# Earlier softmax sums and a copy of h in step 23 of 32: one change to a three-stage kernel on one core

## The chip, the cores and the metric

The kernel runs on one core of a Trainium2 chip. The metric is device time in microseconds (us), the median of several runs. The engines of the core work side by side, each through its own queue in order: TensorE (PE; its weight loads are shown as PEld), VectorE (DVE), ScalarE (ACT), GpSimd (POOL) and SyncE (SP), which issues most of the DMAs. An instruction that waits for a semaphore holds up all that is queued behind it on its engine.

## What is computed

```
# attention: 4 batches, 8 heads, 576 positions, head size 64; float32
scores = q @ k.T / 8                      # heads 0-3: the last 32 positions; heads 4-7: every 32nd
attn   = exp(scores - max); attn /= sum(attn) + 1e-9
x      = attn @ v                         # -> 2304 tokens x 512
# first feed forward
h = x @ w_in;  g = h * cos(h);  x = g @ w_out         # 512 -> 2048 -> 512
# second feed forward
h = x @ w_in2; g = P(h) / Q(h); out = g @ w_out2      # P cubic, Q quadratic
```

## The kernel before

The attention of one batch is cut into two halves of 288 positions, so there are eight halves, n = 0 to 7 in the code (the first to the eighth). Each half has four pairs of heads, i = 0 to 3. The scores of a pair lie on 128 partitions in five blocks: 445 columns in all for pairs 0 and 1, 315 or 630 for pairs 2 and 3 (630 in odd n).

The first feed forward runs in blocks of tokens, and a block in 16 steps, one for each 128 of the 2048 hidden columns. Steps are counted by `g` over the whole kernel; the first feed forward has g = 0 to 127, the second g = 128 to 223. Up to g = 47 the blocks are 256 or 352 tokens wide, from g = 48 on 288. While a block is worked on, the attention of a later half is worked in beside it: half n (from 2 on) has its stages in the steps after `s0 = 16*(n-1)`.

In step g, PE computes h of that step in a PSUM bank (`l1`, L409: 12 matmuls). There are two banks for h, so that L409 of step g+2 needs all readers of the h of step g to be done. Then come the letters of a string that sets the order in which the other engines' instructions are issued; the string of a step is in `ORD` or, for g = 48 to 111, in `C_ORD[g % 32]`. Letters in capitals U, K, V belong to h of step g, and N, M, G, H to step g-1:

- U (L498, ACT): t = h/2pi + 1/4, rounded to an integer. t has two buffers, so that U of step g+2 waits until H of step g has read t.
- K (L504, ACT): `hs`, a copy of h in SBUF; k (L506) does it on DVE. A step without K has none.
- V (L508, DVE): u = h/2pi - t.
- N (L510, ACT): the sine of u. M (L512, DVE): t = u * hs, or u * h, straight from the bank, in a step without a copy.
- G (L516, ACT): gh, the rounded high part of t. H or h (L518, on POOL or on DVE): gl = t - gh.
- T: the transposes (L345, PE) of a pair of heads and their copies `pt` to SBUF (L353, ACT). L: the "late" work planned for this step.

After the letters, PE does the second matmul for step g-3 (`l2`, L428: 12 matmuls, needs gh and gl of that step), and then, for a pair transposed in this step, probabilities times v (`att_o`, L364), which needs `pt`. So PE's queue in a step with a pair is L409, L345, L428, L364.

The late work of a step holds, in this order, decoding of the second feed forward's weights (L143 on ACT, two steps on L596, L157 and L603 on DVE, two instructions each) and then attention: the maximum, the exponential, and the sum and normalisation of a pair. A sum is three instructions on DVE (L287 over the columns, L334 and L335 on five columns), a normalisation one on POOL (L336). The table `TABE` (even n) or `TABO` (odd n), for n from 3 on (n = 2 has a table of its own, `TAB2`), has a row for each pair; its last three entries are the steps, counted from s0, of the exponential, of sum and normalisation, and of transpose and product with v:

```
TABO = [[-4, -2, -1, 0, 4, 9, 11], [-3, -1, 0, 1, 6, 10, 12], [-2, 12, 2, 3, 4, 11, 13], [1, 13, 4, 5, 6, 12, 14]]
```

Five halves use these two tables: n = 3 (sums in steps 41 to 44, transposes in 43 to 46), 4 (57 to 60, 59 to 62), 5 (73 to 76, 75 to 78), 6 (89 to 92, 91 to 94) and 7 (105 to 108, 107 to 110).

Of the kernel before, what the change touches and what calls it, by code (L numbers as in the profile page):

```python
# [45 lines left out]
TAB = ((-4, -2, -1, 0, 6, 9, 11), (-3, -1, 0, 1, 6, 10, 12), (0, 12, 2, 3, 6, 11, 13), (1, 13, 4, 5, 6, 12, 14))  # L46
TAB2 = TABE = TABO = TAB
W2RD = (5, 7, 2)
# [9 lines left out]
C_ORD = {}  # L58
# [22 lines left out]
BLAG = 8  # L81
START = ['cst ACT', 'lq 0 0', 'lq 0 2 ACT', 'load 2 0', 'lv 0 1', 'lv 0 3 w0', 'lq 0 3', 'lq 0 1 ACT', 'load 0 0', 'lv 0 0', 'load 0 1', 'load 1 0 ACT', 'load 1 1', 'warm 38', 'lv 0 2 w0', 'masks', 's 0 0 y', 's 0 1 y', 's 0 2 y', 's 0 3 y', 'lq 1 0', 'ab', 'lq 1 2', 'lq 1 1', 'load 2 1', 'load 3 0', 'load 3 1', 'red 0 0', 'lv 1 0', 'exps 0 0', 'lq 1 3', 'ms 0 1', 'ex 0 1', 'red 0 2', 'lv 1 1', 'exps 0 2', 'norm 0 0 POOL', 'ms 0 3', 'ex 0 3', 'load 4 1', 'sum 0 1', 'norm 0 2 POOL', 'norm 0 1 POOL', 'sum 0 3', 'warm 29', 'abs 0 0', 'abs 0 1', 't 0 0 h', 'load 4 0', 'te 0 0', 'd 0 0 0', 'norm 0 3 POOL', 'o 0 0', 'd 0 1 0', 'd 0 0 1', 'd 0 1 1', 'd 0 0 2', 'd 0 1 2', 't 0 1 y', 'abs 1 1', 'te 0 1', 'oe 0 0', 'split 0 1 POOL', 'abs 1 0', 't 0 2 h', 'o 0 1', 'd 1 1 0', 'd 1 1 1', 'd 1 0 0', 'te 0 2', 'load 6 1', 'd 1 0 1', 'split 0 0 POOL', 'd 1 0 2', 't 0 3 y', 'oe 0 1', 's 1 0 y', 'te 0 3', 'd 1 1 2', 'o 0 2', 'split 1 0 POOL', 'oe 0 2', 'split 1 1 POOL', 'o 0 3', 's 1 1 y', 'abs 2 0', 'abs 2 1 DVE', 'd 2 0 0', 'd 2 1 0', 'abs 3 0', 'd 2 0 1', 'd 2 1 1', 'abs 3 1', 's 1 2 y', 's 1 3 a', 'red 1 0', 'd 2 1 2', 'red 1 1', 'd 2 0 2', 'exps 1 0', 'oe 0 3', 'split 2 0 POOL', 'exps 1 1', 'red 1 2', 'split 2 1 POOL', 'd 3 1 0', 'red 1 3', 'exps 1 2', 'exps 1 3', 'd 3 0 0', 'd 3 0 1', 'd 3 1 1', 'd 3 0 2', 'd 3 1 2', 'split 3 0 POOL', 'load 5 0', 'load 5 1', 'load 7 0', 'split 3 1 POOL DVE', 'load 7 1', 'load 6 0', 'next']
LV1 = [2, 4]
TABE = [[-5, -2, -1, 0, 4, 9, 11], [-3, -1, 0, 1, 6, 10, 12], [0, 12, 2, 3, 6, 11, 13], [1, 13, 4, 5, 6, 12, 14]]
TABO = [[-4, -2, -1, 0, 4, 9, 11], [-3, -1, 0, 1, 6, 10, 12], [-2, 12, 2, 3, 4, 11, 13], [1, 13, 4, 5, 6, 12, 14]]
C_ORD.update({0: 'swNMUKjVGHTL', 1: 'swNMUjVGhTL', 2: 'swNMUKjVGhTL', 3: 'swNMUKjVGhTL', 4: 'swNMUKjVGhTL', 5: 'swNMUKjVGhTL', 6: 'swNMUKjVGhTL', 7: 'swNMUkjVGHTL', 8: 'swNMUKjVGHTL', 9: 'swNMUKjVGHTL', 10: 'swNMUKJVGhTL', 11: 'swNMUKjVGhTL', 12: 'swNMUKjVGhTL', 13: 'swNMUKjVGhTL', 14: 'swNMUKjVGHTL', 15: 'swNMUKjVGHTL', 16: 'swNMUKjVGHTL', 17: 'swNMUKjVGhTL', 18: 'swNMUKjVGhTL', 19: 'swNMUKjVGhTL', 20: 'swNMUKjVGHTL', 21: 'swNMUKjVGhTL', 22: 'swNMUKjVGhTL', 23: 'swNMUjVGhTL', 24: 'swNLMUKjVGHT', 25: 'wNsMUKjVGHTL', 26: 'swNMUKjVGhTL', 27: 'swNMUKjVGhTL', 28: 'swNMUKjVGhTL', 29: 'swNMUKjVGhTL', 30: 'swNMUKjVGHTL', 31: 'swNMUKjVGHTL'})
W2RD = [4, 6, 2]
X2RD = [4, 2, 2]

# [2 lines left out]
def attention_moe_moe_kernel(ctx: ExitStack, tc: tile.TileContext, qk0, qk, vv, w1, w2, consts, a, b, out):  # L92
# [455 lines left out]
    def plan(kind, g, fn, *args):  # L548
        plans[kind].setdefault(g, []).append((fn, args))
# [5 lines left out]
    def plan_attention(p):  # L555
        for n in range(1, 2 * B):
            s0 = NF * (n - 1)
            if n == 1:
# [6 lines left out]
                continue  # L565
            for i, (lq, lv, ss, ms, xs, us, ts) in enumerate(TAB2 if n == 2 else (TABE, TABO)[n % 2]):
                if lq is not None:
# [164 lines left out]
    with tc.manual_schedule():  # L732
        with tc.tile_pool(name="att", bufs=2) as p:
# [87 lines left out]
            for kind, g, cmd in PL1:  # L821
                plan(kind, g, do, cmd)
            plan("late", 2 * NF + TABO[0][4], roots)
            plan_w2(p)
# [98 lines left out]
```

## Time and profile before

| what | us |
|---|---|
| median of three runs (972.56 to 974.1) | 972.74 |
| the profiled execution, its own time | 970.86 |
| span of that execution in the trace | 969.1 |
| PE busy | 917.1 (95%) |
| DVE busy | 712.1 (73%) |
| ACT busy | 690.8 (71%) |
| POOL busy | 291.5 (30%) |

The span is the stretch from the first to the last instruction that the trace shows. PE is busy nearly all of it, and its granted clock is full (a nine or more in tenths) from the second of 40 slices on. The shares are means over stages: the start up to about 90 us, the first feed forward with attention beside it to about 545 us, the second feed forward after it.

### The profile page before, as it was taken

How to read it: one execution, taken by the hardware profiler on the slowest of the kernel's cores; microseconds unless marked ns; L12 is line 12 of the kernel's file. 1: busy time of each engine (PE TensorE's matmuls, PEld its weight loads, DVE VectorE, ACT ScalarE, POOL GpSimd, SP SyncE). 2: the span in 40 equal slices, each digit the busy share in tenths (PEclk: the TensorE clock that was granted, in tenths of full speed). 3: DMA queues.
4: the chain of work that ended last, by engine and by line, in shares of the span. 5: the costliest groups of instructions: out<-in, count | busy, mean ns of one | idle time of the engine just before them, and what ended most of it. 6: DMA issues, size and time to landing. Idle time of an engine off the chain costs nothing.

```text
span 969.1 us, 17280 instructions
## 1 busy us (share of the span) xinstructions
PE 917.1 (95%) x6367; PEld 857.2 (88%) x6367; DVE 712.1 (73%) x1337; ACT 690.8 (71%) x1453; POOL 291.5 (30%) x279
## 2 busy tenths in 40 slices
PE   7578999999999999999999999999999999999997
PEld 6467999989989989999899988898898898898895
DVE  5998745685665676656758788778778787787776
ACT  5987765665674865657658877777777777777875
POOL 2577722132222122221313123232232233232221
PEclk9799999999999999999999999999999999999999
DMA  9766103434324344344236320010100200100000
GB/s 312 265 222 211 45 2 119 163 107 150 113 101 154 104 144 141 131 146 139 93 104 190 120 73 0 12 55 1 58 9 1 66 1 1 66 1 0 33 1 33
DMA packets 51525, 89.35 MB, mean 92 GB/s; under 512 B 4584, under 2 KB 28400, under 8 KB 51440
## 3 DMA queue, kind: packets, MB, share of 16 engines
q1 hardware_dynamic: 50720, 86.58, 27.2%
q10 hardware_dynamic: 720, 1.67, 0.5%
q8 instruction: 50, 0.82, 0.3%
q14 instruction: 35, 0.29, 0.1%
HBM read 70.40 MB, written 17.83 MB: 91 GB/s over the span
## 4 chain that ended last, share of the span: by engine, by line
PE 38%; DVE 22%; ACT 21%; POOL 11%; issue 5%; DMA 2%; POOLq 0%; SPq 0%; ACTq 0%; DVEq 0%
PE h L409 17%; PE y L428 16%; POOL z L468 9%; DVE r L471 7%; ACT r L467 6%; ACT r L466 5%; ACT gh L477 5%; DVE h L472 3%; DVE a L472 3%; PE a L249 2%; DVE dec L157 2%; PE a L364 2%; DMA qk<-in_qk_dram 2%; PE a L345 1%; DVE t L512 1%
## 5 line engine op out<-in xcount | busy, mean ns | idle before, releaser
L409 PE MATMUL h<-xh,w 128*128 128x288 f32 (+3 forms) x1408 | 338.6, 312 | 14.1 <-DVE t L512 11.8
L409 PEld LDWEIGHTS h<-xh,w 128*128 128x128 f32 x1408 | 245.3, 191 | 19.3 <-DVE t L512 13.1
L428 PE MATMUL y<-gh,w 128*128 128x288 f32 (+2 forms) x1024 | 229.1, 300 | 0.6 <-ACT w L163 0.6
L409 PE MATMUL h<-xl,w 128*128 128x288 f32 (+3 forms) x704 | 207.1, 310 | 0.0
L428 PE MATMUL y<-w,gh 128*128 128x512 f32 x576 | 195.9, 393 | 5.5 <-DVE ev L442 4.6
L468 POOL TENSOR_TENSOR z<-q,r 128x384 f32<-128x384 f32 x96 | 97.3, 1013 | 297.9 <-ACT r L467 287.8
L428 PEld LDWEIGHTS y<-gh,w 128*128 128x128 f32 x1024 | 172.0, 189 | 0.8 <-ACT w L163 0.8
L428 PE MATMUL y<-gl,w 128*128 128x288 f32 (+2 forms) x512 | 151.6, 296 | 2.2 <-POOL gl L518 2.1
L409 PEld LDWEIGHTS h<-xl,w 128*128 128x128 f32 x704 | 134.8, 191 | 1.8
L428 PEld LDWEIGHTS y<-w,gh 128*128 128x128 f32 x576 | 108.1, 188 | 28.0 <-DVE ev L442 7.1
L471 DVE SCALAR_TENSOR_TENSOR r<-z,r 128x384 f32<-128x384 f32 x96 | 69.5, 724 | 73.9 <-POOL z L468 73.9
L518 POOL TENSOR_TENSOR gl<-t,gh 128x288 fp32r<-128x288 f32 (+2 forms) x67 | 67.2, 1003 | 184.5 <-ACT gh L516 162.4
L498 ACT ACTIVATE t<-h,biases 128x288 int32<-128x288 f32 (+2 forms) x116 | 57.6, 497 | 89.1 <-PE h L409 78.7
L428 PE MATMUL y<-w,gl 128*128 128x512 f32 x288 | 114.7, 398 | 5.1 <-DVE gl L482 5.0
L508 DVE SCALAR_TENSOR_TENSOR u<-h,t 128x288 f32<-128x288 f32 (+2 forms) x128 | 58.2, 455 | 76.5 <-ACT hs L504 60.8
L409 PE MATMUL a<-xh,w 128*128 128x384 f32 x384 | 106.3, 337 | 0.0
L428 PEld LDWEIGHTS y<-gl,w 128*128 128x128 f32 x512 | 97.0, 189 | 3.0 <-POOL gl L518 2.9
L516 ACT ACTIVATE gh<-t 128x288 fp32r<-128x288 f32 (+2 forms) x128 | 56.6, 442 | 29.3 <-DVE t L512 27.4
L510 ACT ACTIVATE u<-u,biases 128x288 f32<-128x288 f32 (+2 forms) x128 | 67.8, 530 | 12.9 <-DVE u L508 12.6
L409 PEld LDWEIGHTS a<-xh,w 128*128 128x128 f32 x384 | 70.5, 188 | 1.8
L428 PEld LDWEIGHTS y<-w,gl 128*128 128x128 f32 x288 | 54.0, 188 | 20.0 <-DVE gl L482 12.0
L512 DVE TENSOR_TENSOR t<-u,hs 128x288 f32<-128x288 f32 (+1 forms) x91 | 50.5, 555 | 25.6 <-ACT u L510 25.1
(115 smaller groups left out, 1601.1 us busy)
## 6 DMA issues: line engine op xcount, KB each, us to landing
raw<-in_w_dram SPq DMA_DIRECT2D x63, 512.0 KB
qk<-in_qk_dram SPq DMA_DIRECT2D x18, 481.0 KB
wf<-dec SPq DMA_DIRECT2D x32, 256.0 KB
wf<-wf SPq DMA_DIRECT2D x32, 256.0 KB
x2s<-x2d SPq DMA_DIRECT2D x24, 192.0 KB
out_dram<-ev SPq DMA_DIRECT2D x17, 256.0 KB
v<-in_vv_dram SPq DMA_DIRECT2D x16, 240.0 KB
v<-in_vv_dram SPq DMA_DIRECT2D x24, 157.5 KB
```

Of the source, the lines that this page charges most:

```text
L409: PE.matmul(h[:, :n], w[d["ph"], f, 0][:, 128 * c:128 * c + 128], x[c][:, cs], start=k == 0, stop=k == len(ops) - 1)
L428: PE.matmul(y, l, r, start=first and i == 0 and bk != bB, stop=last and i == 2 and bk != bA)
L467: ACT.activation(out=r, in_=r, func=AF.Exp, scale=-1.0, bias=biases[:, 1:2])
L468: POOL.tensor_tensor(out=z, in0=q, in1=r, op=ALU.mult)
L471: DVE.scalar_tensor_tensor(out=r, in0=z, scalar=2.0, in1=r, op0=ALU.subtract, op1=ALU.mult, reverse0=True)
L472: DVE.scalar_tensor_tensor(out=h, in0=h, scalar=ab[:, 0:1], in1=r, op0=ALU.add, op1=ALU.mult)
L498: ACT.activation(out=k, in_=h, func=AF.Identity, scale=INV_2PI, bias=biases[:, 2:3])
L508: DVE.scalar_tensor_tensor(out=u, in0=h, scalar=INV_2PI, in1=k, op0=ALU.mult, op1=ALU.subtract)
L510: ACT.activation(out=u, in_=u, func=AF.Sin, scale=TWO_PI, bias=biases[:, 3:4])
L512: DVE.tensor_tensor(out=t, in0=u, in1=e.get("hs", h), op=ALU.mult)
L516: ACT.activation(out=e["gh"], in_=t, func=AF.Copy)
L518: (POOL if c == "H" else DVE).tensor_tensor(out=e["gl"], in0=t, in1=e["gh"].bitcast(F32), op=ALU.subtract)
```

## The change

Two things are changed, both in tables that set the order; no instruction is added but one copy in each of two steps.

```diff
-TABE = [[-5, -2, -1, 0, 4, 9, 11], [-3, -1, 0, 1, 6, 10, 12], [0, 12, 2, 3, 6, 11, 13], [1, 13, 4, 5, 6, 12, 14]]
-TABO = [[-4, -2, -1, 0, 4, 9, 11], [-3, -1, 0, 1, 6, 10, 12], [-2, 12, 2, 3, 4, 11, 13], [1, 13, 4, 5, 6, 12, 14]]
+TABE = [[-5, -2, -1, 0, 4, 7, 11], [-3, -1, 0, 1, 6, 8, 12], [0, 12, 2, 3, 6, 9, 13], [1, 13, 4, 5, 6, 10, 14]]
+TABO = [[-4, -2, -1, 0, 4, 7, 11], [-3, -1, 0, 1, 6, 8, 12], [-2, 12, 2, 3, 4, 9, 13], [1, 13, 4, 5, 6, 10, 14]]
 C_ORD.update({
...
-  23: 'swNMUjVGhTL',
+  23: 'swNMUKjVGhTL',
...
 })
```

The sixth entry of each row falls by two: 20 sums and 20 normalisations (five halves, n = 3 to 7, of four pairs) are issued two steps sooner, while exponentials and transposes stay. `C_ORD[23]` is used at g = 55 and g = 87 alone, the only steps with g % 32 = 23 between 48 and 111; step 119 has a string of its own in `ORD`.

VectorE in half n = 5, from V of step 71 on. Before:

```order
L508 SCALAR_TENSOR_TENSOR u<-h,t 128x288
L512 TENSOR_TENSOR t<-u,hs 128x288
L508 SCALAR_TENSOR_TENSOR u<-h,t 128x288
L596 TENSOR_SCALAR dec<-dec 128x512 x2
L157 SCALAR_TENSOR_TENSOR dec<-raw,dec 128x512 x2
L512 TENSOR_TENSOR t<-u,hs 128x288
L508 SCALAR_TENSOR_TENSOR u<-h,t 128x288
L603 SCALAR_TENSOR_TENSOR dec<-raw,dec 128x512 x2
L287 TENSOR_REDUCE sm<-p 128x5
L334 TENSOR_SCALAR sm<-sm 128x5
L335 RECIPROCAL sm<-sm 128x5
```

After, from the same V of step 71 on:

```order
L508 SCALAR_TENSOR_TENSOR u<-h,t 128x288
L287 TENSOR_REDUCE sm<-p 128x5
L334 TENSOR_SCALAR sm<-sm 128x5
L335 RECIPROCAL sm<-sm 128x5
L512 TENSOR_TENSOR t<-u,hs 128x288
L508 SCALAR_TENSOR_TENSOR u<-h,t 128x288
L596 TENSOR_SCALAR dec<-dec 128x512 x2
L157 SCALAR_TENSOR_TENSOR dec<-raw,dec 128x512 x2
L287 TENSOR_REDUCE sm<-p 128x5
L334 TENSOR_SCALAR sm<-sm 128x5
L335 RECIPROCAL sm<-sm 128x5
```

The sums of pairs 0 and 1, which stood behind the L603 pair and one step later, now stand in front of M of step 71 and of M of step 72; those of pairs 2 and 3 take their old places in steps 73 and 74. Half n = 7 has the same order.

VectorE in half n = 4, from the weight decoding of step 56 on. Before:

```order
L596 TENSOR_SCALAR dec<-dec 128x512 x2
L157 SCALAR_TENSOR_TENSOR dec<-raw,dec 128x512 x2
L512 TENSOR_TENSOR t<-u,h 128x288
L508 SCALAR_TENSOR_TENSOR u<-h,t 128x288
L512 TENSOR_TENSOR t<-u,hs 128x288
```

After, from the first sum, which is issued at the end of step 55, on:

```order
L287 TENSOR_REDUCE sm<-p 128x5
L334 TENSOR_SCALAR sm<-sm 128x5
L335 RECIPROCAL sm<-sm 128x5
L596 TENSOR_SCALAR dec<-dec 128x512 x2
L157 SCALAR_TENSOR_TENSOR dec<-raw,dec 128x512 x2
L287 TENSOR_REDUCE sm<-p 128x5
L334 TENSOR_SCALAR sm<-sm 128x5
L335 RECIPROCAL sm<-sm 128x5
L512 TENSOR_TENSOR t<-u,hs 128x288
```

M of step 55 reads the copy `hs` in place of the bank `h`, and has two sums in front of it (step 56 has L ahead of M in its string, so its decoding and its sum come first). Half n = 6, step 87, has the same order.

GpSimd in half n = 5, a piece of the difference:

```order
-L518 TENSOR_TENSOR gl<-t,gh 128x288 x3
-L336 TENSOR_TENSOR p<-p,sm 128x445 x2
+L518 TENSOR_TENSOR gl<-t,gh 128x288
+L336 TENSOR_TENSOR p<-p,sm 128x445
+L518 TENSOR_TENSOR gl<-t,gh 128x288
+L336 TENSOR_TENSOR p<-p,sm 128x445
+L518 TENSOR_TENSOR gl<-t,gh 128x288
```

The normalisations of pairs 0 and 1 now stand between the gl of steps 70, 71 and 72 instead of behind all three.

## Rows read from the trace of the kernel before

**Rows 1.** The page, first part: busy us (share of the span) x instructions.

```profile
PE 917.1 (95%) x6367; PEld 857.2 (88%) x6367; DVE 712.1 (73%) x1337; ACT 690.8 (71%) x1453; POOL 291.5 (30%) x279
```

**Rows 2.** Waits of PE, 200 to 545 us: who waited for whom, total us, times, longest.

```profile
PE h L409 <- DVE t L512: 3.8, 2, 1.9
PE a L345 <- POOL p L336: 2.7, 2, 1.4
...
PE a L364 <- ACT pt L353: 1.0, 1, 1.0
```

**Rows 3.** Timeline, half 3: start us, length us, instruction [idle before it, releaser].

```profile
218.68 1.24 POOL L336 TENSOR_TENSOR p<-p,sm 128x630 f32<-128x630 f32 x1 [1.93 <-DVE sm L335]
219.88 1.23 POOL L518 TENSOR_TENSOR gl<-t,gh 128x352 fp32r<-128x352 f32 x1
...
221.14 0.56 ACT L498 ACTIVATE t<-h,biases 128x352 int32<-128x352 f32 x1 [2.96 <-POOL gl L518]
...
222.85 0.80 PE L364 MATMUL a<-pt,v 89*64 89x58 f32 x20 [1.02 <-ACT pt L353]
```

**Rows 4.** Timeline of PE, half 4: first L409 of step 57, and L364 of pair 0.

```profile
274.14 0.40 PE L409 MATMUL h<-xh,w 128*128 128x288 f32 x1 [1.89 <-DVE t L512]
...
284.40 0.80 PE L364 MATMUL a<-pt,v 89*64 89x58 f32 x20
```

**Rows 5.** Timeline of PE, half 5: transposes of pair 0 and its L364.

```profile
344.91 0.78 PE L345 MATMUL a<-cst,p 128*89 128x128 f32 x5 [1.36 <-POOL p L336]
...
347.39 0.80 PE L364 MATMUL a<-pt,v 89*64 89x58 f32 x20
```

**Rows 6.** Timeline of DVE, half 5 (the first row from step 68).

```profile
321.95 0.76 DVE L596 TENSOR_SCALAR dec<-dec 128x512 int32<-128x512 int32 x2
...
336.59 0.46 DVE L512 TENSOR_TENSOR t<-u,hs 128x288 f32<-128x288 f32 x1 [1.31 <-ACT u L510]
...
337.65 1.37 DVE L596 TENSOR_SCALAR dec<-dec 128x512 int32<-128x512 int32 x2
...
342.69 0.60 DVE L287 TENSOR_REDUCE sm<-p 128x5 f32<-128x445 f32 x1
...
343.64 0.43 DVE L512 TENSOR_TENSOR t<-u,hs 128x288 f32<-128x288 f32 x1
...
346.05 0.43 DVE L512 TENSOR_TENSOR t<-u,hs 128x288 f32<-128x288 f32 x1
...
347.51 0.80 DVE L287 TENSOR_REDUCE sm<-p 128x5 f32<-128x630 f32 x1
...
348.67 0.46 DVE L376 TENSOR_TENSOR xl<-a,xh 128x288 fp32r<-128x288 f32 x1
349.10 1.33 DVE L512 TENSOR_TENSOR t<-u,hs 128x288 f32<-128x288 f32 x1
```

**Rows 7.** Timeline of ACT, half 5: copies pt of pair 0.

```profile
346.87 0.74 ACT L353 ACTIVATE pt<-a 89x384 f32<-89x384 f32 x2
```

**Rows 8.** Timeline of POOL, half 5: one gl, and the normalisation of pair 2.

```profile
337.70 1.02 POOL L518 TENSOR_TENSOR gl<-t,gh 128x288 fp32r<-128x288 f32 x1 [1.76 <-PE h L409]
...
348.88 1.24 POOL L336 TENSOR_TENSOR p<-p,sm 128x630 f32<-128x630 f32 x1 [1.61 <-DVE sm L335]
```

**Rows 9.** Timeline of DVE, half 4: steps 56 and 57.

```profile
271.53 0.98 DVE L596 TENSOR_SCALAR dec<-dec 128x512 int32<-128x512 int32 x2
...
273.64 0.45 DVE L512 TENSOR_TENSOR t<-u,h 128x288 f32<-128x288 f32 x1
...
276.93 0.46 DVE L508 SCALAR_TENSOR_TENSOR u<-h,t 128x288 f32<-128x288 f32 x1 [1.11 <-ACT hs L504]
```

**Rows 10.** Timeline of POOL and ACT, half 4: gl of 55, U of 57, pt of pair 0.

```profile
274.69 0.81 POOL L518 TENSOR_TENSOR gl<-t,gh 128x288 fp32r<-128x288 f32 x1 [9.47 <-ACT gh L516]
...
276.09 0.50 ACT L498 ACTIVATE t<-h,biases 128x288 int32<-128x288 f32 x1 [1.07 <-PE h L409]
...
283.41 0.75 ACT L353 ACTIVATE pt<-a 89x384 f32<-89x384 f32 x2
```

More of the change, by code (lines that the diff above doesn't have):

```diff
@@ L83 @@
 LV1 = [2, 4]
-TABE = [[-5, -2, -1, 0, 4, 9, 11], [-3, -1, 0, 1, 6, 10, 12], [0, 12, 2, 3, 6, 11, 13], [1, 13, 4, 5, 6, 12, 14]]
-TABO = [[-4, -2, -1, 0, 4, 9, 11], [-3, -1, 0, 1, 6, 10, 12], [-2, 12, 2, 3, 4, 11, 13], [1, 13, 4, 5, 6, 12, 14]]
-C_ORD.update({0: 'swNMUKjVGHTL', 1: 'swNMUjVGhTL', 2: 'swNMUKjVGhTL', 3: 'swNMUKjVGhTL', 4: 'swNMUKjVGhTL', 5: 'swNMUKjVGhTL', 6: 'swNMUKjVGhTL', 7: 'swNMUkjVGHTL', 8: 'swNMUKjVGHTL', 9: 'swNMUKjVGHTL', 10: 'swNMUKJVGhTL', 11: 'swNMUKjVGhTL', 12: 'swNMUKjVGhTL', 13: 'swNMUKjVGhTL', 14: 'swNMUKjVGHTL', 15: 'swNMUKjVGHTL', 16: 'swNMUKjVGHTL', 17: 'swNMUKjVGhTL', 18: 'swNMUKjVGhTL', 19: 'swNMUKjVGhTL', 20: 'swNMUKjVGHTL', 21: 'swNMUKjVGhTL', 22: 'swNMUKjVGhTL', 23: 'swNMUjVGhTL', 24: 'swNLMUKjVGHT', 25: 'wNsMUKjVGHTL', 26: 'swNMUKjVGhTL', 27: 'swNMUKjVGhTL', 28: 'swNMUKjVGhTL', 29: 'swNMUKjVGhTL', 30: 'swNMUKjVGHTL', 31: 'swNMUKjVGHTL'})
+TABE = [[-5, -2, -1, 0, 4, 7, 11], [-3, -1, 0, 1, 6, 8, 12], [0, 12, 2, 3, 6, 9, 13], [1, 13, 4, 5, 6, 10, 14]]
+TABO = [[-4, -2, -1, 0, 4, 7, 11], [-3, -1, 0, 1, 6, 8, 12], [-2, 12, 2, 3, 4, 9, 13], [1, 13, 4, 5, 6, 10, 14]]
+C_ORD.update({0: 'swNMUKjVGHTL', 1: 'swNMUjVGhTL', 2: 'swNMUKjVGhTL', 3: 'swNMUKjVGhTL', 4: 'swNMUKjVGhTL', 5: 'swNMUKjVGhTL', 6: 'swNMUKjVGhTL', 7: 'swNMUkjVGHTL', 8: 'swNMUKjVGHTL', 9: 'swNMUKjVGHTL', 10: 'swNMUKJVGhTL', 11: 'swNMUKjVGhTL', 12: 'swNMUKjVGhTL', 13: 'swNMUKjVGhTL', 14: 'swNMUKjVGHTL', 15: 'swNMUKjVGHTL', 16: 'swNMUKjVGHTL', 17: 'swNMUKjVGhTL', 18: 'swNMUKjVGhTL', 19: 'swNMUKjVGhTL', 20: 'swNMUKjVGHTL', 21: 'swNMUKjVGhTL', 22: 'swNMUKjVGhTL', 23: 'swNMUKjVGhTL', 24: 'swNLMUKjVGHT', 25: 'wNsMUKjVGHTL', 26: 'swNMUKjVGhTL', 27: 'swNMUKjVGhTL', 28: 'swNMUKjVGhTL', 29: 'swNMUKjVGhTL', 30: 'swNMUKjVGHTL', 31: 'swNMUKjVGHTL'})
 W2RD = [4, 6, 2]
```

## Prediction

> **What bounds the kernel now.** PE is busy for 95% of the span [rows 1], so the first view to read is what PE waited for in the stretch that the change touches, 200 to 545 us [rows 2]. Five waits there can be moved by it: two of L409 for M (L512), 3.8 us together, two of the transposes L345 for the normalisation on POOL, 2.7 us, and one of L364 for its copies pt, 1.0 us. The timelines then tell where each lies. (Halves are named by the code's n.) In half 3 it is the L364 of pair 1 [rows 3]; in halves 4 and 6 the L409 of steps 57 and 89 [rows 4]; in halves 5 and 7 the transposes of pair 0 [rows 5]. Together 1.0 + 3.8 + 2.7 = 7.5 us, which is the most that the change can gain. The next view is the timeline of DVE at the same places, since both edits alter what is queued there. In half 5 it goes without a gap from 337.65 us to 349.10 us: M of step 73 at 343.64, M of step 74 at 346.05, and the copies pt of pair 0 follow M of step 74 by 0.82 us, because in ACT's queue they stand behind G of step 74 [rows 6, 7]. PE's L364 starts 0.52 us after these copies start [rows 5, 7]. So at this place two chains run side by side to the same L364: POOL's normalisation, which is late, and DVE's queue, which is hardly earlier.
>
> **The price of a sum.** From its L287 to the next instruction on DVE a sum takes 343.64 - 342.69 = 0.95 us for 445 columns and 348.67 - 347.51 = 1.16 us for 630 [rows 6]. The sums of 315 columns in even halves I take at the nearest row, 0.95 us less 0.1. None is added; what counts is which M they are put in front of.
>
> **The copy.** One more L504 on ACT in steps 55 and 87. It frees the h bank at V instead of at M, so the wait of 1.89 us [rows 4] goes. Its own price, about 0.3 us on ACT, is hidden: M of step 55, which waits for what is behind it on ACT, is late by more for another reason (below).
>
> **Half 3.** The wait of 1.02 us comes from POOL: gl of step 42 at 219.88 stood behind a normalisation that ran from 218.68 to 219.92, and U of step 44 waited 2.96 us for that gl; the copies pt, and with them L364, are queued behind [rows 3]. After the change this normalisation is issued two steps sooner, gl no longer has its 1.24 us in front of it, and U and the copies can come sooner by about that, more than the 1.02 us that PE waits. The sums go into steps 39 to 42, where DVE still has idle time. I count -1.0 us; bounds 0 and -1.02.
>
> **Halves 5 and 7, step by step.** The normalisation of pair 0 will be done several us ahead (two steps, at 3 us each), so the transposes no longer wait: -1.36 us at L345. But L364 behind them still needs the copies, these need G, and that needs M of step 74. Before, M of step 74 had two sums of pairs 0 and 1 in front of it within DVE's gapless stretch (2 x 0.95). After, four sums are in front of it. The first falls into the idle 1.31 us before M of step 71 [rows 6], the other three do not: 0.95 + 1.16 + 1.16 = 3.27 us against 1.90 us. M of step 74, its G, the copies and L364 come 1.37 us later, L364 at 348.76 us instead of 347.39. PE waits there for the copies; the time saved at L345 is inside that wait, and the net is **+1.37 us** if nothing else is lost. That is the lower bound.
>
> To it comes what DVE and POOL take from each other. M at 349.10 took 1.33 us instead of 0.43 to 0.46, and it ended just after the normalisation that ran on POOL from 348.88 to 350.12; the L596 pair took 1.37 us beside a gl on POOL (337.70 to 338.72), and 0.76 us without one [rows 6, 8]. So an instruction of DVE that meets one on POOL loses some 0.6 to 0.9 us. After the change the first normalisation starts about 336.4 us and meets M of step 71 at 336.6, which is then held for about the rest of it, some 0.75 us; DVE had 1.06 us from that M to its L596 pair, for two instructions of which V needs 0.46 us at most, so I leave 0.45 us of it. The other moved normalisations stand beside L603 and beside gl of step 73 on DVE; I count one further loss of 0.6 us. That gives 1.37 + 0.45 + 0.6 = **+2.4 us** for each of the two halves. If each meeting costs in full it is +2.8 us. The value taken lies nearer the upper end because the rows show the loss at every meeting that I looked at.
>
> The Trainium skill states a rule for this (SBUF — State Buffer, section "SBUF: two separate sides"): VectorE and GpSimd share a pair of SBUF ports by an exclusive lock, which a VectorE instruction with two SBUF inputs needs too, and the one that comes second is held for the whole of the first. By that rule alone each meeting costs in full, +2.8 us here and +1.3 us in halves 4 and 6, and the whole sum would be +7.2 us, 979.9 us; with no such lock it would be the lower ends, 975.4 us. The trace agrees where it can: M with u and hs both in SBUF was held to the end of the normalisation, 1.33 us.
>
> **Halves 4 and 6, step by step.** M of step 55 was at 273.64 us [rows 9]. After, two sums stand in front of it, 1.90 us, of which 0.22 us falls into the wait for ACT that is inside the 0.98 us of the L596 pair (0.76 us without): +1.68 us. M's result goes on through G on ACT, gl on POOL (274.69 + 0.81 = 275.50 us, 1.86 us after M) and then U of step 57, which needs the buffer t that gl reads, and V of step 57, 0.84 us after U [rows 9, 10]. So V of step 57 cannot come sooner than about 2.75 us after M of step 55: 273.64 + 1.68 + 2.75 = 278.07 us, against 276.93 us before [rows 9], +1.14 us. From there to M of step 58 the same work is queued (sums of 315 in place of 445 columns, -0.2 us), so that the copies pt, at 283.41 us before [rows 10], come at 284.35 us and L364 0.52 us later, at 284.87 us against 284.40 us [rows 4]. The wait of 1.89 us is gone and yet the net is **+0.5 us**: PE waits at L364, in part already at L409 of step 58 for V of step 56, which also stands behind both sums. If the L596 pair meets the normalisation of pair 0 (+0.6 us) and gl of step 55 waits 0.2 us behind that of pair 1, it is +1.3 us. Taken: **+1.0 us** each, nearer the upper end for the same reason. A lower bound far off is -1.89 us, if V of step 57 did not depend on M of step 55 in this way.
>
> After these places nothing follows: in the steps up to the next half PE had no waits, and DVE has two sums less in the steps that come behind, so a delay of PE stays as it is. DMAs are not moved; in SP's queue only names of buffers differ.
>
> **Sum.** -1.0 + 2 x 1.0 + 2 x 2.4 = +5.8 us. On the profiled execution: 970.86 + 5.8 = 976.7 us. The median of the three runs is 1.9 us above that execution, and I put the sum on the median: 972.74 + 5.8 = 978.5 us. With all lower ends: -1.0 + 1.0 + 2.7 = +2.7 us, 975.4 us. With all upper ends, half 3 at nothing: 2.6 + 5.6 = +8.2 us, 980.9 us.
>
> **Rivals.**
> *All five waits go and nothing comes instead*: -7.5 us, 965.2 us. This is what holds if DVE has enough slack to take the sums sooner. For it: DVE is busy for only 73% of the span [rows 1], and half 3 is such a place. Against it: DVE's queue in half 5 has no gap for eleven us, and L364 waits for the copies whatever the normalisation does.
> *The copy pays, the sums at best break even*: in halves 4 and 6 the idle time of DVE around V of step 57 (1.11 us before it [rows 9]) takes the sums, and -3.8 us is kept; in halves 5 and 7 the wait only changes its place, from L345 to L364, at the same end. -1.0 - 3.8 + 0 = -4.8 us, 967.9 us. It decides for faster if M of step 74 comes no later than before, that is, if three sums cost no more there than two did. For it: before the change the L596 and L603 pairs lose time to POOL already, and this could go away.
> *Little net*: halves 5 and 7 at +1.4 us, halves 4 and 6 at 0, half 3 -1.0 us: +1.7 us, 974.4 us.
> That the change does not do what it says is excluded by the order of the instructions; it does less in one respect, since step 23 of 32 occurs only twice.
>
> **How the numbers follow.** A measurement of this kernel can tell about 0.2%, 1.95 us, from no change. Forecast, slower by more than that: 0.75. Little net: 0.11. Copy pays: 0.08. All gained: 0.06. So faster 0.14, same 0.11, slower 0.75. The range reaches from just below the rival at 967.9 us to 981.5 us, a little above the sum of the upper ends; outside it lies the rival at 965.2 us and what of the forecast goes beyond.
>
> **What the profile of the changed kernel would show.** Waits of PE: none for L512 and none for the normalisation L336, and in their place waits of L364 for ACT's pt, about 3.8 us (2.4 + 1.36) in halves 5 and 7 each, and waits of L409 for DVE's V (L508) and of L364 for pt in halves 4 and 6, about 2.9 us together in each. On DVE four sums end before M of step 74, and some M (L512) beside a normalisation take over a microsecond. In half 3 no wait of L364. I am wrong if L364 in halves 5 and 7 waits less than 1.4 us (then M of step 74 was not late), or if PE waits at neither place.

## The result, and the profile after

The changed kernel takes 981.79 us (median of five runs, 980.79 to 982.67) where the kernel before takes 972.56 us beside it: 1.0094 times as long, 95% interval 1.0080 to 1.0108, or +9.2 us. Slower was forecast, at +5.8 us with an upper end of 981.5 us; the measured time lies 0.3 us above that end. The profiled execution took 980.79 us, its span is 979.0 us.

What PE waited for from 200 to 560 us in the kernel after (total us, times, longest), in answer to [rows 2]:

```profile
PE a L364 <- ACT pt L353: 9.6, 4, 3.5
PE h L409 <- DVE u L508: 4.3, 4, 1.4
PE a L249 <- DVE t L512: 0.3, 1, 0.3
```

The waits for M (L512 at L409) and for the normalisation (L336 at L345) are gone, and the copies pt (L353) have taken their place, with V (L508) at L409. Of the 4.3 us, 1.4 us are the wait ahead of the first moved sum, which was there before. Where the waits lie is shown by the timeline of PE after, in halves 3, 4 and 5, in answer to [rows 3 to 5]:

```profile
221.43 0.80 PE L364 MATMUL a<-pt,v 89*64 89x58 f32 x20
...
275.34 0.40 PE L409 MATMUL h<-xh,w 128*128 128x288 f32 x1 [1.36 <-DVE u L508]
...
283.84 0.80 PE L364 MATMUL a<-pt,v 89*64 89x58 f32 x20 [1.34 <-ACT pt L353]
...
343.13 0.71 PE L345 MATMUL a<-cst,p 128*89 128x128 f32 x5
...
348.87 1.32 PE L364 MATMUL a<-pt,v 89*64 89x58 f32 x20 [3.45 <-ACT pt L353]
...
350.53 0.44 PE L409 MATMUL h<-xl,w 128*128 128x288 f32 x1
...
353.17 1.27 PE L345 MATMUL a<-cst,p 128*89 128x128 f32 x5
```

In half 3 L364 of pair 1 has no wait left. In half 4 one wait of 1.89 us has become two, 1.36 and 1.34 us. In half 5 the transposes no longer wait and L364 does, for 3.45 us. And then something that no term of the prediction held: the same twenty L364 take 1.32 us in place of 0.80 us, and an L409 of 288 columns 0.44 us in place of 0.29 us. The windows of this stretch give the reason (us; busy us of PE, PEld, DVE, ACT and POOL with their instructions; PEclk, the granted clock; DMA share; GB/s):

```profile
345.00:349.00 4.00, 0.55 (x6) 0.32 (x6) 3.65 (x9) 2.70 (x7) 2.39 (x2) 0.86 0.99 339
349.00:351.00 2.00, 2.00 (x23) 1.90 (x24) 0.70 (x2) 0.85 (x3) 0.07 (x1) 0.50 0.29 115
...
353.20:356.00 2.80, 2.80 (x18) 2.77 (x17) 0.82 (x2) 2.59 (x7) 0.00 (x0) 0.73 0.05 12
356.00:360.00 4.00, 4.00 (x46) 3.80 (x45) 1.28 (x4) 2.37 (x7) 0.00 (x0) 1.00 0.37 100
```

PE comes out of its wait at a granted clock of 0.50, the lower of the two levels (1.2 GHz), and is back at 1.00 only about six us later (354.6 us, from the lengths of the matmuls). From L364 of pair 0 to L364 of pair 1 it took 352.03 - 347.39 = 4.64 us before and takes 356.14 - 348.87 = 7.27 us now: 2.6 us more. In half 7 it is 488.88 - 481.28 = 7.60 us against 4.65 us, 2.95 us more.

The whole account comes from the start of the last L364 of each half, before and after:

| half | before | after | behind by | made in this half | forecast |
|---|---|---|---|---|---|
| (first L364 of half 3) | 216.45 | 216.12 | -0.33 | | |
| 3 | 233.49 | 232.06 | -1.43 | -1.10 | -1.0 |
| 4 | 298.29 | 297.72 | -0.57 | +0.86 | +1.0 |
| 5 | 361.34 | 365.40 | +4.06 | +4.63 | +2.4 |
| 6 | 424.76 | 429.92 | +5.16 | +1.10 | +1.0 |
| 7 | 487.76 | 498.14 | +10.38 | +5.22 | +2.4 |

The five halves add up to +10.7 us. With the -0.3 us ahead of them and -0.5 us behind them this is the difference of the two spans, 979.0 - 969.1 = 9.9 us, where the medians differ by 9.2 us.

In half 5, 3.45 - 1.36 = 2.09 us of the 4.63 us is longer waiting, and the other 2.5 us is the lower clock. In half 7 the waits at L409 and L364 give 0.25 + 3.47 - 1.36 = 2.36 us, and the clock 2.9 us.

DVE after, half 5, in answer to [rows 6], with two normalisations from POOL's timeline; behind it, from ACT's timeline, the copies:

```profile
334.26 0.45 DVE L508 SCALAR_TENSOR_TENSOR u<-h,t 128x288 f32<-128x288 f32 x1
334.63 0.61 DVE L287 TENSOR_REDUCE sm<-p 128x5 f32<-128x445 f32 x1
...
336.02 0.46 DVE L512 TENSOR_TENSOR t<-u,hs 128x288 f32<-128x288 f32 x1
336.07 1.20 POOL L336 TENSOR_TENSOR p<-p,sm 128x445 f32<-128x445 f32 x1 [0.40 <-DVE sm L335]
...
341.30 2.27 DVE L603 SCALAR_TENSOR_TENSOR dec<-raw,dec 128x512 int32<-128x512 int32 x2
343.48 0.80 DVE L287 TENSOR_REDUCE sm<-p 128x5 f32<-128x630 f32 x1
...
344.86 1.30 POOL L336 TENSOR_TENSOR p<-p,sm 128x630 f32<-128x630 f32 x1 [1.84 <-DVE sm L335]
345.57 0.90 DVE L518 TENSOR_TENSOR gl<-t,gh 128x288 fp32r<-128x288 f32 x1
346.39 0.80 DVE L287 TENSOR_REDUCE sm<-p 128x5 f32<-128x630 f32 x1
...
347.54 0.43 DVE L512 TENSOR_TENSOR t<-u,hs 128x288 f32<-128x288 f32 x1
...
348.35 0.74 ACT L353 ACTIVATE pt<-a 89x384 f32<-89x384 f32 x2
```

M of step 74 (347.54) comes behind four sums, the copies 0.81 us behind it, L364 0.52 us behind these, as forecast. In half 4 the chain M, G, gl, U, V of steps 55 to 57 runs as forecast too, at DVE and ACT:

```profile
274.50 0.42 DVE L512 TENSOR_TENSOR t<-u,hs 128x288 f32<-128x288 f32 x1
...
276.50 0.51 ACT L498 ACTIVATE t<-h,biases 128x288 int32<-128x288 f32 x1 [0.65 <-POOL gl L518]
...
277.34 0.46 DVE L508 SCALAR_TENSOR_TENSOR u<-h,t 128x288 f32<-128x288 f32 x1 [0.56 <-ACT hs L504]
```

V of step 57 comes 2.84 us after M of step 55 (2.75 us in the prediction, and 0.2 us for a normalisation in front of gl).

### The profile page after: what moved, and what is told of

The parts are those of the page before. It is cut to its first block, busy times and chain, and to the rows that moved or that the text cites. A ratio compares the mean times of both kernels' runs of the same rounds, so it can differ in the third digit from the quotient of the medians.

```text
span 979.0 us, 17265 instructions
## 1 busy us (share of the span) xinstructions
PE 922.3 (94%) x6367; PEld 862.5 (88%) x6367; DVE 714.3 (73%) x1337; ACT 691.7 (71%) x1455; POOL 292.1 (30%) x279
## 4 chain that ended last, share of the span: by engine, by line
PE 36%; DVE 24%; ACT 22%; POOL 10%; issue 5%; DMA 1%; POOLq 0%; SPq 0%; DVEq 0%; ACTq 0%
PE h L409 16%; PE y L428 14%; POOL z L468 9%; DVE r L471 7%; ACT r L467 6%; ACT r L466 5%; ACT gh L477 5%; DVE h L472 3%; DVE a L472 3%; DVE dec L157 2%; PE a L249 2%; PE a L364 2%; DMA raw<-in_w_dram 1%; PE a L345 1%; DVE t L512 1%
## 5 line engine op out<-in xcount | busy, mean ns | idle before, releaser
L409 PE MATMUL h<-xh,w 128*128 128x288 f32 (+3 forms) x1408 | 340.3, 313 | 13.7 <-DVE t L512 8.6
L409 PEld LDWEIGHTS h<-xh,w 128*128 128x128 f32 x1408 | 246.3, 192 | 19.4 <-DVE t L512 9.3
L409 PE MATMUL h<-xl,w 128*128 128x288 f32 (+3 forms) x704 | 207.6, 311 | 0.0
L409 PEld LDWEIGHTS h<-xl,w 128*128 128x128 f32 x704 | 135.4, 192 | 1.8
L518 POOL TENSOR_TENSOR gl<-t,gh 128x288 fp32r<-128x288 f32 (+2 forms) x67 | 66.6, 995 | 191.5 <-ACT gh L516 173.9
L508 DVE SCALAR_TENSOR_TENSOR u<-h,t 128x288 f32<-128x288 f32 (+2 forms) x128 | 58.2, 455 | 79.0 <-ACT hs L504 63.7
L409 PE MATMUL a<-xh,w 128*128 128x384 f32 x384 | 106.2, 337 | 0.0
L409 PEld LDWEIGHTS a<-xh,w 128*128 128x128 f32 x384 | 70.5, 188 | 1.8
L512 DVE TENSOR_TENSOR t<-u,hs 128x288 f32<-128x288 f32 (+1 forms) x93 | 49.2, 529 | 21.5 <-ACT u L510 20.9
```

The lines of the kernel that those rows point to most:

```text
L409: PE.matmul(h[:, :n], w[d["ph"], f, 0][:, 128 * c:128 * c + 128], x[c][:, cs], start=k == 0, stop=k == len(ops) - 1)
L508: DVE.scalar_tensor_tensor(out=u, in0=h, scalar=INV_2PI, in1=k, op0=ALU.mult, op1=ALU.subtract)
L512: DVE.tensor_tensor(out=t, in0=u, in1=e.get("hs", h), op=ALU.mult)
L518: (POOL if c == "H" else DVE).tensor_tensor(out=e["gl"], in0=t, in1=e["gh"].bitcast(F32), op=ALU.subtract)
```

## The experiments

The theory: the copies pt, queued behind M of step 74, make PE wait in the odd halves, and a wait of that length costs once more through the clock behind it. Rivals are named with each run. All times are medians; the kernel before took 972.35 us beside four of the runs (PE filled, the copies ahead, the copy alone, the sums alone), 972.56 us beside the next four (no normalisations, halves 5 and 7 alone, halves 4 and 6 alone, the first version that gains) and 972.82 us beside the last two.

**PE filled with work in the wait.** The changed kernel, with matmuls into the next step's h bank (overwritten by that step):

```diff
+            if g in (75, 107):
+                state["hb"] = bank("h")
+                for _ in range(24):
+                    PE.matmul(state["hb"][:, :HS], wh[1, f, 0][:, :128], xh[0][:, ...], start=True, stop=True)
             run("pe2", g)
...
-        h = bank("a" if d["ph"] == 2 and f % 2 else "h")
+        h = state.pop("hb", None) or bank("a" if d["ph"] == 2 and f % 2 else "h")
```

> The changed kernel, with 24 matmuls of 288 columns into the h bank of the next step ahead of L364 of pair 0 in steps 75 and 107, so that PE works through most of its wait for the copies. Theory (after the wait of 3.45 us PE runs at half the clock for some 6 us, which costs 2.5 to 2.9 us in each half): granted clock 1.00 through 348 to 356 us, and 5.0 us less in all, 976.8 us. Rival (PE is slow there for another reason, such as the DMA traffic of 339 GB/s in the same stretch): the clock stays at 0.50 and the time at 981.8 us or above.

976.32 us, 1.0044 of before (1.0027 to 1.0060), 5.5 us less than the changed kernel (5.3 us, if each is set against the kernel before that ran beside it), though PE does 48 matmuls more. The timeline of PE in this kernel, with the new matmuls at L728:

```profile
346.30 3.47 PE L728 MATMUL h<-xh,w 128*128 128x288 f32 x24
349.70 0.80 PE L364 MATMUL a<-pt,v 89*64 89x58 f32 x20
```

and its windows, with the columns as above:

```profile
345.00:349.00 4.00, 3.93 (x30) 3.70 (x29) 3.72 (x11) 1.88 (x5) 1.72 (x2) 1.00 0.92 310
349.00:353.00 4.00, 4.00 (x46) 3.77 (x45) 1.94 (x4) 2.43 (x7) 0.89 (x1) 1.00 0.54 197
```

L364 starts as late as before behind its transposes (349.70 - 343.94 = 5.76 us, against 348.87 - 343.13 = 5.74 us), but the clock stays at 1.00 and the L364 take 0.80 us. The DMA traffic of the same stretch is there in both, 310 against 339 GB/s, so it is not what slowed PE. By the starts of L364, halves 5 and 7 make +2.07 and +2.31 us here, which is the longer waiting (2.09 and 2.36 us) without the rest. The clock's share in the loss is shown.

**The copies ahead in ACT's queue.** The changed kernel with another order in steps 75 and 107:

```diff
-  11: 'swNMUKjVGhTL'
+  11: 'swTNMUKjVGhL'
```

> The changed kernel, with the transposes and copies pt ahead of N, M and G in the order of steps 75 and 107. Theory (L364 waits for M of step 74 only because the copies are queued behind G of step 74): the two waits of 3.45 us and the slow stretches behind them go, 12 us less if nothing else is late, 969.5 us. Rival (VectorE itself cannot keep up there): the wait moves to L409 for V or to L428 for gl, and 2 us or more of each stay, 973.5 us or above.

973.21 us, 1.0005 of before (0.9995 to 1.0015): 8.6 us less than the changed kernel, not 12. The clock stays at 1.00. The timeline of PE:

```profile
346.90 0.80 PE L364 MATMUL a<-pt,v 89*64 89x58 f32 x20 [0.52 <-ACT pt L353]
...
350.75 0.45 PE L345 MATMUL a<-cst,p 128*89 128x128 f32 x2 [0.94 <-DVE xl L376]
```

The wait at L364 falls from 3.45 to 0.52 us, so the queueing behind G and M was its cause. The rival is half right: VectorE is still late, though at neither place that the rival names; 0.94 us of waiting come back one step later, at the transposes of pair 1, for an instruction of DVE (L376) that reads the bank they need. With the 0.52 us that is 1.46 us in each half, 2.9 of the 3.4 us by which the theory is missed.

**Without the normalisations of halves 5 and 7.** The changed kernel; `att_norm` leaves out POOL's instruction there, so these probabilities stay unnormalised:

```diff
+        if n in (5, 7):
+            return
         mul.tensor_tensor(out=pv, in0=pv, in1=sm[:, 8:8 + NBLK]...
```

> The changed kernel without the normalisations on POOL in halves 5 and 7 (left out: the rows of these probabilities are not divided by their sums); the sums stay. Theory (VectorE loses 1.1 us before M of step 74 to the normalisations that run beside it): the wait at L364 falls from 3.45 to about 2.4 us; 979.6 us if the clock still falls behind it, 974.5 us if it does not. Rival (VectorE is late by its own four sums alone): the wait stays at 3.4 us and the time at 981.8 us.

979.44 us, 1.0070 of before (1.0054 to 1.0086), 2.3 us below the changed kernel. The two intervals overlap, so the reading rests on the rows. PE in half 5 of this kernel (its line numbers are two higher from the edit on, so L366 is L364 and L411 is L409):

```profile
351.47 0.80 PE L366 MATMUL a<-pt,v 89*64 89x58 f32 x20 [2.65 <-ACT pt L355]
...
352.60 0.44 PE L411 MATMUL h<-xl,w 128*128 128x288 f32 x1
```

and DVE in the same half (L605 is L603, L520 is L518):

```profile
344.69 1.90 DVE L605 SCALAR_TENSOR_TENSOR dec<-raw,dec 128x512 int32<-128x512 int32 x2
...
348.61 0.46 DVE L520 TENSOR_TENSOR gl<-t,gh 128x288 fp32r<-128x288 f32 x1
```

The L603 pair falls from 2.27 to 1.90 us and the gl of DVE from 0.90 to 0.46 us, 0.81 us together, and PE's wait from 3.45 to 2.65 us, by 0.80 us. So what DVE loses beside POOL's normalisations reaches PE in full. The Trainium skill states a rule for this (SBUF — State Buffer, section "SBUF: two separate sides"): a VectorE instruction with two SBUF inputs is held while a GpSimd instruction has the shared ports. The trace agrees: the gl at 345.57 of the changed kernel ended 0.31 us after the normalisation that had begun before it (344.86 + 1.30 = 346.16 us). After this wait of 2.65 us the granted clock still went down: L364 takes 0.80 us, as before, but the L409 behind it take 0.44 us. That is the branch at 979.6 us of the expectation, yet that the median comes so near to it is in part luck. From L364 of pair 0 to that of pair 1 it takes 6.17 us here, so the clock costs 1.5 us in place of 2.6 us, and halves 5 and 7 make +2.7 us each, 4.4 us less than in the changed kernel in all. In the profiled execution most of that is lost ahead of the changed halves: the first L364 of half 3 comes at 219.57 us instead of 216.12.

**Each part by itself.** The sums of halves 5 and 7 alone (a table of its own for n = 3, with the old values, and `TABE` and `C_ORD` as before):

> Only the sums of halves 5 and 7 sooner; no copy in step 23 of 32, half 3 and the even halves as before. Theory (nearly all of the loss is made here: 2.1 to 2.4 us of longer waiting and 2.6 to 2.9 us at half the clock, in each): +9.9 us, 982.2 us. Rival (the loss needs the even halves' delay too): +5 us, 977.5 us.

983.16 us, 1.0113 of before (1.0094 to 1.0131): +10.6 us. The wait at L364 of half 5 is the same (L365 here is L364, L354 is L353, L410 is L409, L513 is L512):

```profile
273.77 0.40 PE L410 MATMUL h<-xh,w 128*128 128x288 f32 x1 [1.90 <-DVE t L513]
...
274.60 0.44 PE L410 MATMUL h<-xl,w 128*128 128x288 f32 x1
...
350.83 1.32 PE L365 MATMUL a<-pt,v 89*64 89x58 f32 x20 [3.45 <-ACT pt L354]
```

By the starts of L364, halves 5 and 7 make +4.70 and +5.07 us, the +9.9 us of the theory. But halves 4 and 6, which nothing was changed in, make +1.56 and +1.27 us: the waits of 1.90 and 1.89 us at L409 of steps 57 and 89 stand there as in the kernel before, and behind them the granted clock was at 0.50 for 3.2 us each time, which it was not in the profile of the kernel before (1.00 from 274 to 280 us, with the wait of [rows 4]).

The copy of h and the sums of halves 4 and 6 (`TABE` of after, `C_ORD[23]` of after, `TABO` of before):

> The copy of h and the sums of halves 4 and 6 sooner; halves 3, 5 and 7 as before. Theory (two waits of 1.35 us at L409 and L364 in place of one of 1.89 us): +0.9 us each, 974.2 us. Rival (the copy pays all the same): 968.8 to 971 us.

973.54 us, 1.0014 of before (1.0003 to 1.0025): +1.0 us, where +1.8 us was expected, and no gain from the copy. Both together with half 3 give 10.6 + 1.0 - 1.1 = +10.5 us against +9.2 us measured. Intervals of 1.1 to 1.9 us to either side allow that, and the lower clock in halves 4 and 6 of the run before this one, which the changed kernel does not have, is a loss of the right sign and of more than that size. The copy alone:

```diff
-  23: 'swNMUjVGhTL'
+  23: 'swNMUKjVGhTL'
```

> The copy of h in steps 55 and 87 alone, sums at their old steps. Theory (two chains meet at L364 of pair 0): the waits of 1.9 us of L409 of steps 57 and 89 go, but V of step 57 can come only about 2.75 us after M of step 55, so the copies pt of pair 0 come only about 0.5 us sooner and L364 keeps about half of the gain: near -1.0 us for each of the halves 4 and 6, 970.6 us. Rival (the wait was all there was to lose): -3.8 us, 968.8 us.

969.52 us, 0.9975 of before (0.9963 to 0.9988): -2.8 us, between the two expectations; the interval holds the theory's -2.0 us. By the starts of L364, halves 4 and 6 make -1.08 and -1.04 us, the size of the theory; where the other 0.7 us of the median come from is not shown. PE in half 4 of this kernel:

```profile
280.47 0.78 PE L345 MATMUL a<-cst,p 128*89 128x128 f32 x5 [0.71 <-POOL p L336]
```

The wait of 1.89 us is gone and 0.71 us of it comes back at the transposes, which wait for the normalisation. The theory had the size, but the meeting point wrong: it is not the copies but the normalisation that is next late there. The sums alone, without the copy:

> The sums two steps sooner alone, step 23 of 32 without its copy. Theory: the h bank of step 55 is freed by M of step 55, which now stands behind two sums, at about 275 us instead of 270.7; L409 of step 57 waits some 4.3 us, and if a wait of that length halves the granted clock as the 3.45 us in half 5 did, some 2.5 us more follow: 987 to 991 us. Rival (the copy makes no difference once the sums are moved): 982 us.

988.05 us, 1.0161 of before (1.0145 to 1.0177): +15.7 us, within the theory's bounds. PE in half 4:

```profile
275.08 0.61 PE L409 MATMUL h<-xh,w 128*128 128x288 f32 x1 [4.07 <-DVE t L512]
```

and the window that begins with it:

```profile
275.00:278.00 3.00, 2.92 (x12) 2.92 (x13) 1.26 (x3) 0.91 (x2) 1.55 (x2) 0.50 0.00 0
```

So the two edits belong together: with the sums in front of it, M of step 55 frees the bank so late that PE waits 4.07 us for it, unless step 23 of 32 has its copy; and here too the clock was at 0.50 behind the wait, with no DMA traffic at all beside it. What that cost differs: from waits of 4.07 and 4.03 us, halves 4 and 6 make +3.49 and +5.04 us, 1.3 and 2.9 us more than the waits have grown.

**A version that gains.** The copy of h, half 3 as changed, and of halves 5 and 7 only pair 0 sooner:

```diff
-TABO = [[-4, -2, -1, 0, 4, 9, 11], ...
+TABO = [[-4, -2, -1, 0, 4, 7, 11], ...            # n = 5, 7; the other rows as before
+TAB3 = ...                                        # n = 3: TABO of the changed kernel
```

> The copy of h, all four sums of half 3 sooner, and of halves 5 and 7 only the sum and normalisation of pair 0; the sums of halves 4 and 6 at their old steps. Theory: pair 0's sum falls into idle time of VectorE, its normalisation is done before the transposes, and M of step 74 has one sum less in front of it (0.95 us), so the wait of 1.36 us at L345 shrinks by about 1.0 us in each of the two halves. With -1.1 us of half 3 and -2.8 us as the copy alone gave: -5.9 us, 966.5 us. Rival (the wait moves whole to L364, as it did with all sums sooner): -3.9 us, 968.5 us.

967.76 us, 0.9952 of before (0.9938 to 0.9967): -4.8 us, between theory and rival. By the starts of L364, halves 5 and 7 make -0.81 and -0.77 us (-1.0 in the theory, nothing in the rival). PE's waits in it (L365 is L364, L354 is L353, L346 is L345, L337 is L336):

```profile
PE a L365 <- ACT pt L354: 1.8, 2, 0.9
PE a L346 <- POOL p L337: 1.4, 2, 0.7
```

The sum in the idle time of step 71 is free: in the changed kernel M of step 71 comes 1.76 us after V (336.02 - 334.26), as before (336.59 - 334.83). 0.9 us of waiting stays at L364 in the odd halves and 0.7 us at L345 in the even ones. Then the copies ahead in steps 75 and 107 (`11: 'swTNMUKjVGhL'`):

> As the kernel with only pair 0 of halves 5 and 7 sooner, and in steps 75 and 107 the transposes and copies pt stand ahead of N, M and G. Theory: the wait of 0.9 us at L364 in each of the two halves goes, since the copies no longer wait for M of step 74: 1.8 us less, 966.0 us. Rival (the wait moves on to the transposes of pair 1, as with all sums sooner, 0.9 us each): 967.8 us.

966.25 us, 0.9933 of before (0.9921 to 0.9946), 1.5 us less; the waits of 0.9 us at L364 of pair 0 are gone, and 0.18 us is left in each half at L364 of pair 1. Last, pair 0 of halves 4 and 6 one step sooner, and the copies ahead in steps 59 and 91:

```diff
-TABE = [[-5, -2, -1, 0, 4, 9, 11], ...
+TABE = [[-5, -2, -1, 0, 4, 8, 11], ...
-  27: 'swNMUKjVGhTL'
+  27: 'swTNMUKjVGhL'
```

> The same, and in halves 4 and 6 the sum and normalisation of pair 0 one step sooner, with the transposes and copies ahead of N, M and G in steps 59 and 91. Theory: the wait of 0.7 us at L345 in each even half goes as well, and V of steps 56 and 57, 0.95 us later, is still in time: 964.6 us. Rival (that delay of V makes L409 of step 58 or 59 wait, as with all sums sooner): 966 us or more.

963.95 us, 0.9914 of before (0.9900 to 0.9928): -8.9 us, and 17.8 us less than the changed kernel. Its waits of PE, 195 to 560 us:

```profile
PE h L410 <- DVE u L509: 1.4, 1, 1.4
PE y L429 <- DVE ev L443: 0.8, 1, 0.8
PE a L365 <- ACT pt L354: 0.4, 2, 0.2
```

and the window of 200 to 540 us:

```profile
200.00:540.00 340.00, 338.63 (x2804) 333.17 (x2805) 236.96 (x477) 230.69 (x511) 82.60 (x79) 1.00 0.42 138
```

None of the five waits of before is left (the 0.4 us are at L364 of pair 1; the other two waits were there before), and PE is busy for 338.6 of 340 us at the full clock.

## Why the prediction fell short

The way and the places were right, the size was not: +9.2 us for +5.8 us, and outside the range.

- *Half 3*, -1.0 us: -1.10 us, the wait of 1.02 us gone.
- *Halves 4 and 6*, +1.0 us each: +0.86 and +1.10 us. The wait of 1.89 us went, and 1.36 us at L409 of step 58 for V and 1.34 us at L364 for pt came; the prediction named both places. V of step 57 followed M of step 55 by 2.84 us (2.75 us).
- *Halves 5 and 7*, +2.4 us each: the waits alone, 2.09 and 2.36 us, confirm the queue arithmetic. M of step 74 came 13.28 us after V of step 71 (347.54 - 334.26), before 11.22 us (346.05 - 334.83), so it is 2.06 us late: 1.37 us by the count of sums, and 0.69 us beside POOL. These are the rows of the kernel before, from the timelines of DVE and POOL:

```profile
334.83 0.45 DVE L508 SCALAR_TENSOR_TENSOR u<-h,t 128x288 f32<-128x288 f32 x1
...
340.87 1.89 DVE L603 SCALAR_TENSOR_TENSOR dec<-raw,dec 128x512 int32<-128x512 int32 x2
...
343.87 0.99 POOL L336 TENSOR_TENSOR p<-p,sm 128x445 f32<-128x445 f32 x1 [1.65 <-DVE sm L335]
...
344.58 0.59 DVE L518 TENSOR_TENSOR gl<-t,gh 128x288 fp32r<-128x288 f32 x1
```

- The 0.69 us are the L603 pair, 2.27 us instead of 1.89, and gl, 0.90 us instead of 0.59. The prediction put this at 1.05 us, of which 0.45 us at M of step 71; but in half 5 that M, which began 0.05 us before the normalisation, was not held (0.46 us at 336.02). In half 7 its counterpart began 0.21 us behind a normalisation (468.22 against 468.01) and took 1.03 us. That the rows showed a loss "at every meeting" was misread: M of step 73 (0.43 us at 343.64) had met the normalisation at 343.87 before the change too, began ahead of it and lost nothing. The two errors, 0.45 us too much at M and 0.1 us too little at L603 and gl, leave 2.06 us against 2.4 us.
- *The step that failed* is the sentence "PE waits there for the copies; the time saved at L345 is inside that wait, and the net is +1.37 us if nothing else is lost", and with it the +2.4 us, which prices the wait at its length. A term is missing: what the wait does to PE itself. The prediction expected about 3.8 us of waiting at L364 (3.45 us measured) and priced it as 3.8 us; the 2.5 and 2.9 us at half the clock behind it were in no term and in neither end of the range. They are 5.4 us of the 10.7 us that the five halves add up to. With them the sum would have been 5.8 + 5.4 = +11.2 us. The kernel with PE filled shows the term by itself: 5.3 to 5.5 us.
- *Where it could have been read.* The trace of before had no wait of 3 us in this stretch, but its start shows the same thing. The granted clock is not full there from the second of the 40 slices on: that slice, 24 to 48 us, reads seven tenths, and a later slice that reads nine hides a stretch at 0.50 from 90 to 92 us. After a wait of 2.09 us an L409 of 256 columns takes 0.41 us there, and 0.28 us a few us later:

```profile
88.35 0.39 PE L428 MATMUL y<-gl,w 128*128 128x256 f32 x1 [2.09 <-POOL gl L518]
...
90.28 0.41 PE L409 MATMUL h<-xh,w 128*128 128x256 f32 x1
...
94.13 0.28 PE L409 MATMUL h<-xh,w 128*128 128x256 f32 x1
```

- *The rivals.* None of the three came. "All five waits go" did go by the letter, since all five left, but others came in their place. What would have been needed is the last kernel: each sum where DVE is idle, and the copies off the chain.
- *The signs to look for* were right but for two: 3.45 us instead of 3.8 us at L364, and an M of over a microsecond beside a moved normalisation in half 7 only, not in half 5.

Open stays why two waits of the same length cost 2.5 and 2.9 us by the clock here, and in other runs 1.6 us (3.43 us of waiting, half 5 of the sums alone), and why a wait of 1.9 us cost nothing in the kernel before and 1.5 us in the run with halves 5 and 7 alone. It was not tried further.

## What to carry to other kernels

When a change puts a wait of several microseconds on a TensorE that has been dense, price the matmuls behind it at the lower clock as well as the wait; here that was as much again as the wait had grown. Before a step is moved sooner, count what stands in front of the next late consumer in each queue, not the work of the step: of the four sums moved in halves 5 and 7, the one that fell into idle time cost nothing and the three others made PE wait. And when two chains end at the same instruction, shorten the later one too, or only the name of the wait changes.

## What the runs showed that was not expected

From 200 us on, the waits of PE of up to 1.44 us, in all these kernels, were followed by the full clock. Waits of 1.9 us were followed by it in the kernel before, but in the run with halves 5 and 7 alone by a granted clock of 0.50 (1.2 GHz) for 3.2 us, which cost 1.5 us each time. Waits of 2.65, 3.45 and 4.07 us between dense stretches were all followed by 0.50 and a way back to 1.00 of three to about six us, at a cost of 1.3 to 2.9 us that does not follow the length of the wait. Matmuls whose result nobody reads, put into the wait, kept the clock at 1.00 and made the kernel 5.3 to 5.5 us faster than the same kernel without them.
